# Causal attention and hard-swish MLP: the first loads in another order, and one small exponential at the start

## The chip, the cores and the metric

The kernel runs on one core of a Trainium2 chip. Its time is the device time of the whole program in microseconds (us). A core has TensorE (PE in the rows; PEld is its weight load), VectorE (DVE), ScalarE (ACT) and GpSimd (POOL), which compute, and SyncE (SP), which here issues every DMA. Each engine takes its instructions in the order in which the program lists them, and waits at the head of its list until the semaphores of that instruction are reached.

## The reference

```python
scores = q @ k^T / sqrt(64)                  # 4 batches, 12 heads, 448 x 64, causal mask
attn   = softmax(scores); x = attn @ v       # x laid out as 1792 tokens x 768
h      = x @ w_in                            # 768 -> 2048
out    = (h * clip(h + 3, 0, 6) / 6) @ w_out # 2048 -> 768
```

All is float32 at the border. The kernel keeps that accuracy by splitting x, the weights and the gated activations into a high and a low part and adding three matmuls (high by high, low by high, high by low).

## The kernel before

The 448 queries of a sequence are cut in four blocks of 112. **Group 0** is the first block of all four batches (448 tokens, made by `first_pair`, two heads at a time, six pairs p0 to p5); groups 1 to 4 are the other 336 queries of each batch (`pair`). Attention of a group must be done before its MLP (`group`). The MLP of a group is a long row of large matmuls on TensorE: 16 chunks of w_in (L598 to L600, 18 matmuls a chunk), then 24 of w_out.

A first pair goes through these steps: mask into two PSUM banks (L322), products of q and k (L329), on VectorE the row maximum of head 1 and of head 0 (L336, L342 between them) and the subtraction for head 0 (L356), on ScalarE the exponentials (L348 four times for head 1, L360 for head 0), on VectorE sum and inverse (L363, L369, L370), on GpSimd the scaling of both heads (L377), on TensorE the turn of both (L386), copies of the turned blocks (L238 on ScalarE or L241 on VectorE), the product with v (L399), and the split of x (L238 twice, then L250).

In group 0 the weights come as 64-bit words. VectorE turns every chunk of w_in (768 columns) into plain numbers in two halves of three instructions (L571, L573, L576) through a scratch PSUM bank; then ScalarE makes the high part (wh, L238), and GpSimd or VectorE the low part (wl, L250). The pairs of batch 0 in `pair` begin with their scores on TensorE (L453: two of 448 columns, two of 336, two of 224), each into a PSUM bank of its own, and then L476 on VectorE.

The order of all this is set by a planner in the kernel (`Flow.run`): each operation has a key (its due time, smaller first), estimated lengths and the buffers that it needs, and whenever an engine is free the planner gives it the ready operation with the smallest key. What comes out is one fixed list for each engine. PSUM has six banks tagged "s" (scores, attention, conversion scratch) and two tagged "mo" (turns, MLP sums). The DMAs of the first loads have keys from -900 on, so that they come first; equal keys go in the order in which they were written.

Of the kernel before, what the change touches and what calls it, by code (L numbers as in the profile page):

```python
# [32 lines left out]
F32 = mybir.dt.float32  # L33
F32R = mybir.dt.float32r
I32 = mybir.dt.int32
ACTF = mybir.ActivationFunctionType
# [154 lines left out]
def tile_causal_attention_hardswish_moe(ctx: ExitStack, tc: tile.TileContext, q, k, v, w_in, w_out, out):  # L191
    nc = tc.nc
# [12 lines left out]
    def buf(tag, shape, dt=F32):  # L205
        return Buf(tag, shape, dt)
# [4 lines left out]
    def ap(b):  # L211
        if b.tile is None:
            b.tile = pools[b.tag].tile(b.shape, b.dt, tag=b.tag, name=b.tag)
        return b.tile

    def f(x):
        return x.bitcast(F32)
# [35 lines left out]
    const = pools["const"]  # L253
# [2 lines left out]
    mask = const.tile([C, S], F32, tag="mask", name="mask")  # L256
    maskr = const.tile([C, B, C], F32R, tag="maskr", name="maskr")
    three = const.tile([128, 1], F32, tag="three", name="three")

    def setup():  # L260
        nc.vector.memset(ident, 1.0)
        nc.vector.memset(mask, 0.0)
        nc.vector.memset(three, 3.0)
        nc.gpsimd.affine_select(
            out=ident, in_=ident, pattern=[[-1, C]], base=0, channel_multiplier=1,
            compare_op=ALU.is_equal, fill=0.0,
        )
        nc.gpsimd.affine_select(
            out=mask[:, R:], in_=mask[:, R:], pattern=[[-1, C]], base=0, channel_multiplier=1,
            compare_op=ALU.is_ge, fill=-8.0e9,  # L270
        )
        nc.vector.tensor_copy(identr, ident)
        nc.vector.tensor_copy(maskr, mask[:, R:].unsqueeze(1).to_broadcast([C, B, C]))
# [17 lines left out]
    first_qk = buf("gh", [128, 2 * NPAIR, S])  # L291
    first_v = buf("gl", [128, NPAIR, S + 64])

    def by_batch(x):
        return x.rearrange("m (b s) -> m b s", b=B)

    def first_pair(p):
        t = T_FIRST + 8 * p
        for a, src in enumerate((q, k)):
            dma(  # L300
                -900 + 4 * p, 230e3, lambda a=a: by_batch(ap(first_qk)[:, 2 * p + a]),
                lambda src=src: src[:, p, :, :, :C].rearrange("b e d s -> (e d) b s"),
                w=[(first_qk, p, a)],
            )
# [239 lines left out]
    def cols(i):  # L544
        return 768 if i < NF else 512

    def weights(g, i, t, early):

        n = cols(i)
        wd, wh, wl = buf("wd", [128, 1536], I32), buf("wh", [128, 768], F32R), buf("wl", [128, 768], F32R)  # L550
        if g:
            dma(t - T_W - T_WLOAD, 512 * n, lambda: f(ap(wd))[:, :n], lambda: kept[i, :, :n], [("kept", i)], [(wd, 0)])
            w, wk = lambda: f(ap(wd))[:, :n], [(wd, 0)]
        else:
            m, r = divmod(i - NF, 4)
            src = w_in[i] if i < NF else w_out[m, :, 4 * r:4 * r + 4]
            dma(
                early if early else t - T_W - T_WLOAD, 1024 * n,
                lambda: ap(wd)[:, :2 * n].rearrange("p (n k) -> p n k", k=256), lambda: src, [], [(wd, 0)],
            )  # L560
            wf = buf("op", [128, 768])
            w = lambda: ap(wf)[:, :n]

            def bits(cv, o, m, step):
                ti = ap(cv)[:, :m].bitcast(I32)
                low, high = (ap(wd)[:, 2 * o + a:2 * o + 2 * m:2] for a in range(2))
                if step == 0:  # L570
                    nc.vector.tensor_scalar(ti, high, 3, 0x3FFFFFFF, ALU.logical_shift_left, ALU.bitwise_and)  # L571
                elif step == 1:
                    nc.vector.scalar_tensor_tensor(ti, high, -(1 << 30), ti, ALU.bitwise_and, ALU.bitwise_or)  # L573
                else:
                    o = ap(wf)[:, o:o + m].bitcast(I32)
                    nc.vector.scalar_tensor_tensor(o, low, 29, ti, ALU.logical_shift_right, ALU.bitwise_or)  # L576

            wk = []
            m = n if n <= 512 else n // 2
            for o in range(0, n, m):  # L580
                cv = bank("s")
                wk.append((wf, o))
                one_by_one = [
                    (elem(m), lambda _, cv=cv, o=o, a=a: bits(cv, o, m, a), [[(cv, 0)], [(cv, 0)], [(wf, o)]][a])
                    for a in range(3)
                ]
                flow.op(t - T_W + .01, {"D": (1, 0)}, one_by_one, [(wd, 0)] + ([("sums", NPAIR - 1)] if i else []))
            dma(t - T_W, 512 * n, lambda: kept[i, :, :n], w, wk, [("kept", i)])
        move(t - T_W + .1, n, lambda: ap(wh)[:, :n], w, wk, [(wh, 0)], {"A": 1})
        minus(  # L590
            t - T_W + .2, n, lambda: ap(wl)[:, :n], w, lambda: f(ap(wh))[:, :n], wk + [(wh, 0)], [(wl, 0)],
            {"D": 1.15, "P": (2, .5)} if g else {"P": 2, "D": (1.15, 2.0)},
        )
        return wh, wl
# [7 lines left out]
    def group(g):  # L602
        n, t0 = (R if g else S), 96 * g
        gh, gl = buf("gh", [128, NF, S], F32R), buf("gl", [128, NF, S], F32R)
        step = 6 * n * .4535e-3
        for i in range(NF):
            t = t0 + 3 * i
            wh, wl = weights(g, i, t, -900 + 4 * i + 11 if not g and i < 4 else None)
            acc, r = bank("mo"), buf("r", [128, S])
            for part in range(3):  # L610
                def products(part=part, wh=wh, wl=wl, acc=acc):
                    for c in (2 * part, 2 * part + 1):
                        xh, xl = (ap(x)[:, :n] for x in x_t[g, c])
                        triple(ap(acc)[:, :n], n, wh, wl, c, xh, xl, c == 0, c == NK - 1)
                cs = (2 * part, 2 * part + 1) if g else range(NK)
                xs = [(x, 0) for c in cs for x in x_t[g, c]]
                pe(t + part, [(step, products, [(acc, 0), ("step", t + part)])], [(wh, 0), (wl, 0)] + xs)
            t -= 4
            one(
                t, {"A": 1}, (n + 300) / 1200,  # L620
                lambda _, r=r, acc=acc: nc.scalar.activation(  # L621
                    ap(r)[:, :n], ap(acc)[:, :n], ACTF.Relu, bias=three, scale=1.0
                ),
                [(acc, 0)], [(r, 0)],
            )
            def gate(_, r=r, acc=acc):
                nc.vector.scalar_tensor_tensor(ap(r)[:, :n], ap(r)[:, :n], 6.0, ap(acc)[:, :n], ALU.min, ALU.mult)  # L627

            one(t, {"D": 1}, elem(n), gate, [(acc, 0)], [(r, 0)])
            move(  # L630
                t, n, lambda i=i: ap(gh)[:, i, :n], lambda r=r: ap(r)[:, :n], [(r, 0)], [(gh, i)],
                {"P": 1.05, "A": (1, .3)} if g else {"A": 1},
            )
            minus(
                t, n, lambda i=i: ap(gl)[:, i, :n], lambda r=r: ap(r)[:, :n], lambda i=i: f(ap(gh)[:, i, :n]),
                [(r, 0), (gh, i)], [(gl, i)], {"D": 1.4, "P": (2.6, 1.0)} if g else {"P": 2.3, "D": (1.4, 1.5)},
            )
        for m in range(NK):
            acc, ob = bank("mo"), buf("r", [128, S])
            for part in range(8):  # L640
                t = t0 + 48 + 8 * m + part
                if part % 2 == 0:
                    wh, wl = weights(g, NF + 4 * m + part // 2, t, None)

                def products(part=part, wh=wh, wl=wl, acc=acc):
                    for i in (2 * part, 2 * part + 1):
                        triple(
                            ap(acc)[:, :n], n, wh, wl, i % 4, ap(gh)[:, i, :n], ap(gl)[:, i, :n], i == 0, i == NF - 1
                        )
                gs = [(x, i) for i in (2 * part, 2 * part + 1) for x in (gh, gl)]  # L650
                pe(t, [(step, products, [(acc, 0), ("step", t)])], [(wh, 0), (wl, 0)] + gs)
            move(
                t + .5, n, lambda ob=ob: ap(ob)[:, :n], lambda acc=acc: ap(acc)[:, :n], [(acc, 0)], [(ob, 0)],
                {"A": 1, "D": (1.1, .5)}, 1.0 / 6.0,
            )
            rows = by_batch(out[128 * m:128 * m + 128])
            if g:
                dma(t + 1, 172e3, lambda rows=rows: rows[:, g - 1, C:], lambda ob=ob: ap(ob)[:, :n], [(ob, 0)])
            else:
                dma(t + 1, 230e3, lambda rows=rows: rows[:, :, :C], lambda ob=ob: by_batch(ap(ob)), [(ob, 0)])  # L660
# [49 lines left out]
```

## Time and profile before

| | us |
|---|---|
| median of 3 runs (lowest to highest) | 661.43 (659.28 to 661.99) |
| the profiled execution | 661.54 |
| its span | 659.8 |
| TensorE busy (share of the span) | 643.9 (98%) |
| VectorE, ScalarE, GpSimd busy | 465.8, 367.3, 301.2 |
| first matmul of group 0's MLP | 45.20 from the start of the span |

Busy times are sums over the span; TensorE has nearly all its idle time ahead of the first matmul of group 0's MLP. In the rows, a timeline line gives start and length, the engine, the line of the kernel, the operation and the tiles; the bracket says how long the engine stood idle before it and what ended the wait. Six q/k/v pair loads of 224 KB each (gh takes q and k, gl takes v) and four weight chunks of 768 KB (wd) are the first 22 transfers.

### The profile page before, as it was taken

To read this page: it belongs to the slowest core of one execution; us is meant where nothing else is said; L and a number is where in the kernel's file an instruction comes from. 1 tells how busy PE (TensorE), PEld (TensorE's weight loads), DVE (VectorE), ACT (ScalarE), POOL (GpSimd) and SP (SyncE) were. 2 spreads that over 40 slices of the span, in tenths; PEclk is the share of its full clock that TensorE was granted. 3 is DMA by queue.
4 is the path that set the end of the run, shared out by engine and by line. 5 is a ranking of instruction groups with operands and counts; after the bars stand their busy time and mean duration, and the time that the engine had idled before them with its cause. 6 is when DMAs were issued, how large, how long until landed. Compare 5 with 4: busy or idle time off the path is not lost.

```text
span 659.8 us, 12245 instructions
## 1 busy us (share of the span) xinstructions
PE 643.9 (98%) x4236; PEld 587.3 (89%) x4236; DVE 465.8 (71%) x939; ACT 367.3 (56%) x870; POOL 301.2 (46%) x333
## 2 busy tenths in 40 slices
PE   7689999999999999999999999999999999999998
PEld 5569887878889999999999999999999999999997
DVE  4889898977687798854588795567798743566432
ACT  3665656654546666555576664656666554444342
POOL 1667667546572686423375563433676410011100
PEclk9979999999999999999999999999999999999999
DMA  9989876888788543556744547555553334643452
GB/s 232 259 267 298 265 242 192 260 282 295 206 265 246 158 144 107 159 171 182 217 152 135 154 127 206 157 168 186 161 168 87 112 113 132 209 139 110 139 164 65
DMA packets 66878, 120.89 MB, mean 183 GB/s; under 512 B 16896, under 2 KB 33408, under 8 KB 66816
## 3 DMA queue, kind: packets, MB, share of 16 engines
q1 hardware_dynamic: 66816, 120.11, 60.7%
q8 instruction: 33, 0.54, 0.3%
q14 instruction: 29, 0.24, 0.1%
HBM read 101.99 MB, written 18.09 MB: 182 GB/s over the span
## 4 chain that ended last, share of the span: by engine, by line
PE 92%; DVE 3%; DMA 1%; SPq 1%; ACT 1%; POOL 1%; issue 1%; DVEq 0%; ACTq 0%; POOLq 0%
PE mo L598 24%; PE mo L600 23%; PE mo L599 23%; PE s L535 6%; PE s L516 6%; PE s L450 3%; PE s L451 2%; PE s L453 2%; DMA gh<-in_k_dram 1%; SPq L229 1%; PE s L399 1%; DVE s L571 1%; DVE s L573 1%; DVE op L576 0%; PE s L329 0%
## 5 line engine op out<-in xcount | busy, mean ns | idle before, releaser
L250 DVE TENSOR_TENSOR wl<-wd,wh 128x512 fp32r<-128x512 f32 (+1 forms) x159 | 142.8, 898 | 99.8 <-ACT wh L238 99.5
L238 ACT CAST wh<-wd 128x512 fp32r<-128x512 f32 (+1 forms) x160 | 112.9, 706 | 120.0 <-PE mo L599 85.9
L598 PE MATMUL mo<-xh,wh 128*128 128x336 f32 (+1 forms) x480 | 160.8, 335 | 0.1
L598 PE MATMUL mo<-gh,wh 128*128 128x336 f32 (+1 forms) x480 | 159.2, 332 | 0.0
L600 PE MATMUL mo<-xh,wl 128*128 128x336 f32 (+1 forms) x480 | 157.2, 327 | 0.0
L600 PE MATMUL mo<-gh,wl 128*128 128x336 f32 (+1 forms) x480 | 156.9, 327 | 0.3 <-POOL wl L250 0.3
L599 PE MATMUL mo<-gl,wh 128*128 128x336 f32 (+1 forms) x480 | 156.4, 326 | 0.0
L599 PE MATMUL mo<-xl,wh 128*128 128x336 f32 (+1 forms) x480 | 156.2, 325 | 0.0
L505 POOL TENSOR_SCALAR pr<-pr,prow 112x224 f32<-112x224 f32 x144 | 109.0, 773 | 39.5 <-DVE prow L493 39.3
L476 DVE CUSTOM_DVE_ANT_0 s<-s,mask 112x448 f32<-112x448 f32 (+1 forms) x144 | 70.6, 527 | 39.7 <-PE s L451 33.1
L245 POOL TENSOR_SCALAR gh<-r 128x336 fp32r<-128x336 f32 x51 | 33.3, 654 | 138.2 <-DVE r L627 128.6
L598 PEld LDWEIGHTS mo<-xh,wh 128*128 128x128 f32 x480 | 91.0, 190 | 5.8 <-issue 1.7
L598 PEld LDWEIGHTS mo<-gh,wh 128*128 128x128 f32 x480 | 90.3, 188 | 2.8 <-issue 0.8
L599 PEld LDWEIGHTS mo<-xl,wh 128*128 128x128 f32 x480 | 91.4, 190 | 1.1
L600 PEld LDWEIGHTS mo<-gh,wl 128*128 128x128 f32 x480 | 90.2, 188 | 2.2 <-POOL wl L250 0.6
L600 PEld LDWEIGHTS mo<-xh,wl 128*128 128x128 f32 x480 | 90.6, 189 | 1.3
L599 PEld LDWEIGHTS mo<-gl,wh 128*128 128x128 f32 x480 | 90.3, 188 | 1.3
L483 ACT ACTIVATE pr<-s,prow 112x448 f32<-112x448 f32 (+1 forms) x144 | 76.9, 542 | 25.7 <-DVE prow L476 25.7
L250 POOL TENSOR_TENSOR wl<-op,wh 128x512 fp32r<-128x512 f32 (+1 forms) x35 | 53.3, 1522 | 44.1 <-ACT wh L238 34.3
L238 ACT COPY pt<-s 112x336 f32<-112x336 f32 x139 | 53.3, 446 | 26.0 <-PE s L516 25.9
L621 ACT ACTIVATE r<-mo,three 128x336 f32<-128x336 f32 (+1 forms) x80 | 44.7, 558 | 26.4 <-PE mo L600 20.9
L245 POOL TENSOR_SCALAR op<-qk 128x784 fp32r<-128x784 f32 x31 | 30.4, 985 | 57.3 <-PE s L451 54.0
(70 smaller groups left out, 853.6 us busy)
## 6 DMA issues: line engine op xcount, KB each, us to landing
wd<-kept_w SPq DMA_DIRECT2D x64, 384.0 KB, 3.3
wd<-kept_w SPq DMA_DIRECT2D x96, 256.0 KB, 2.7
wd<-in_w_in_dram SPq DMA_DIRECT2D x16, 768.0 KB, 5.7
wd<-in_w_out_dram SPq DMA_DIRECT2D x24, 512.0 KB, 5.2
qk<-in_k_dram SPq DMA_DIRECT2D x84, 112.0 KB, 2.7
qk<-in_q_dram SPq DMA_DIRECT2D x84, 84.0 KB, 2.6
kept_w<-op SPq DMA_DIRECT2D x16, 384.0 KB, 5.7
kept_w<-op SPq DMA_DIRECT2D x24, 256.0 KB, 5.4
```

Of the source, the lines that this page charges most:

```text
L238: nc.scalar.copy(o(), i()) if scale is None else nc.scalar.mul(o(), i(), scale)
L245: nc.gpsimd.tensor_scalar(o(), i(), 1.0, 1.0, ALU.mult, ALU.mult)
L250: (nc.gpsimd if e == "P" else nc.vector).tensor_tensor(o(), a(), b(), ALU.subtract)
L476: lambda _, e=e, i=i, w=w, dst=dst: nc.vector.tensor_tensor_reduce(dst(), dst(), mask[:, S - w:], -0.125, 3.0e38, ALU.add, ALU.min, ap(st) ...
L483: lambda _, e=e, i=i, dst=dst: nc.scalar.activation(ap(pr[e, i]), dst(), ACTF.Exp, bias=ap(st)[:, e, i:i + 1], scale=-1.0, accum_out=ap(st ...
L505: nc.gpsimd.tensor_scalar(x, x, r, 1.0, ALU.mult, ALU.mult)
L516: nc.tensor.transpose(ap(tp)[:C, C * o:C * o + C], ap(pr[e, i])[:, C * j:C * j + C], ident)
L535: nc.tensor.matmul(ap(av)[64 * e:64 * e + 64, R - w:R], ap(vr)[:, j, e, :], ap(ph)[:, o:o + w], start=(j == 0), stop=(j == NC_ - 1),)
L598: nc.tensor.matmul(ps, ap(wh)[:, a], xh, start=start, stop=False)
L599: nc.tensor.matmul(ps, ap(wh)[:, a], xl, start=False, stop=False)
L600: nc.tensor.matmul(ps, ap(wl)[:, a], xh, start=False, stop=stop)
L621: lambda _, r=r, acc=acc: nc.scalar.activation(ap(r)[:, :n], ap(acc)[:, :n], ACTF.Relu, bias=three, scale=1.0),
```

## The change

The loads of q and k of pair p get the key -900 + 4p - 6, so that they stand 6 key units, a pair and a half, ahead of the load of v (-900 + 4p, as before). The four early weight chunks get the keys -883, -875, -871 and -867 in place of -889, -885, -881 and -877. And ScalarE computes one exponential of a 128 x 1 constant at the start, which pulls the load of its function table there.

```diff
+    warm = const.tile([128, 1], F32, tag="warm", name="warm")
 
     def setup():
         nc.vector.memset(three, 3.0)
+        nc.scalar.activation(warm, three, ACTF.Exp)
@@ first_pair: loads of q and k of pair p
-                -900 + 4 * p, 230e3, lambda a=a: by_batch(ap(first_qk)[:, 2 * p + a]),
+                -900 + 4 * p - 6, 230e3, lambda a=a: by_batch(ap(first_qk)[:, 2 * p + a]),
@@ group: key of the load of weight chunk i
-            wh, wl = weights(g, i, t, -900 + 4 * i + 11 if not g and i < 4 else None)
+            wh, wl = weights(g, i, t, -900 + (17 if not i else 21 + 4 * i) if not g and i < 4 else None)
```

The lines of the new file stand two further down than those of the old one (L329 is L331 there, L598 is L600).

Since the planner reads the landing of a load as the time from which work is ready, the lists of all engines change. The first places, on SyncE, are the loads themselves; before:

```order
L229 DMA gh<-in_q_dram 128x4x112
L229 DMA gh<-in_k_dram 128x4x112
L229 DMA gl<-in_v_dram 112x4x128
L229 DMA gh<-in_q_dram 128x4x112
L229 DMA gh<-in_k_dram 128x4x112
L229 DMA gl<-in_v_dram 112x4x128
L229 DMA gh<-in_q_dram 128x4x112
L229 DMA gh<-in_k_dram 128x4x112
L229 DMA gl<-in_v_dram 112x4x128
L229 DMA wd<-in_w_in_dram 128x1536
L229 DMA gh<-in_q_dram 128x4x112
L229 DMA gh<-in_k_dram 128x4x112
```

And now:

```order
L229 DMA gh<-in_q_dram 128x4x112
L229 DMA gh<-in_k_dram 128x4x112
L229 DMA gh<-in_q_dram 128x4x112
L229 DMA gh<-in_k_dram 128x4x112
L229 DMA gl<-in_v_dram 112x4x128
L229 DMA gh<-in_q_dram 128x4x112
L229 DMA gh<-in_k_dram 128x4x112
L229 DMA gl<-in_v_dram 112x4x128
L229 DMA gh<-in_q_dram 128x4x112
L229 DMA gh<-in_k_dram 128x4x112
L229 DMA gl<-in_v_dram 112x4x128
L229 DMA gh<-in_q_dram 128x4x112
```

The k of pairs p1, p2, p3 and p5 was transfer 5, 8, 12 and 20, and is now 4, 7, 10 and 16; weight chunk 0 was transfer 10 and is now 18.

On TensorE the list begins, before, with masks (L322), products (L329) and the turn of pair p0 (L386, its two heads pr_215 and pr_225):

```order
L322 MATMUL s<-maskr,identr 112x448 x6
L329 MATMUL s<-gh 112x112 x16
L322 MATMUL s<-maskr,identr 112x448 x2
L329 MATMUL s<-gh 112x112 x8
L322 MATMUL s<-maskr,identr 112x448 x2
L386 MATMUL mo<-ident,pr_215 112x112 x4
L386 MATMUL mo<-ident,pr_225 112x112 x4
```

Eight products are one pair, so x16 is p0 and p1, and the next eight p2. Now (the same operations at L324, L331 and L388):

```order
L324 MATMUL s<-maskr,identr 112x448 x6
L331 MATMUL s<-gh 112x112 x24
L324 MATMUL s<-maskr,identr 112x448 x2
L331 MATMUL s<-gh 112x112 x8
L324 MATMUL s<-maskr,identr 112x448 x2
L388 MATMUL mo<-ident,pr_225 112x112 x4
L388 MATMUL mo<-ident,pr_227 112x112 x4
```

The products of p3 and the masks of p4 now stand between the products of p2 and the turn of p0. (One set of masks moved from ahead of p2's products to behind them.)

The third place is on TensorE where group 0's MLP begins. Before, its first matmul stands right behind the product with v of the last pair, p5 (s_590):

```order
L399 MATMUL s_590<-pt0_577,gl_144 64x112
L399 MATMUL s_590<-pt0_544,gl_144 64x112
L598 MATMUL mo_624<-xh_323,wh_399 128x448
L599 MATMUL mo_624<-xl_346,wh_399 128x448
L600 MATMUL mo_624<-xh_323,wl_413 128x448
```

Now, with the semaphores that each row waits for (s_584 is the product with v of p5):

```order
L401 MATMUL s_584<-pt0_578,gl_148 64x112
L401 MATMUL s_584<-pt0_553,gl_148 64x112
L455 MATMUL s_609<-qk_186 112x448 [waits DMAHW5_49,DMAHW3_49]
L455 MATMUL s_611<-qk_186 112x448 [waits DMAHW6_49,DMAHW4_49,Activation_49]
L455 MATMUL s_618<-qk_186 112x336 [waits DVE_49,PE_49]
L455 MATMUL s_620<-qk_186 112x336 [waits PE_49,Activation_49]
L455 MATMUL s_626<-qk_186 112x224 [waits Activation_49]
L455 MATMUL s_628<-qk_186 112x224 [waits DVE_49]
L600 MATMUL mo_645<-xh_329,wh_448 128x448
L601 MATMUL mo_645<-xl_344,wh_448 128x448
L602 MATMUL mo_645<-xh_329,wl_473 128x448
```

The six scores of the second pair of batch 0 (L455), which before stood among the matmuls of group 0, have moved ahead of its first one. By the values of the semaphores in the two programs, s_618 waits for the first half, and s_628 for the second half, of the conversion of weight chunk 2 on VectorE, since they take over its PSUM scratch banks (s_593 and s_614). That stands on VectorE, behind the copy of p5's turned block (pt0_553) and chunk 1, as

```order
L241 COPY pt0_553<-mo_536 112x448
L573 TENSOR_SCALAR s_558<-wd_173 128x384
...
L578 SCALAR_TENSOR_TENSOR op_570<-wd_173,s_576 128x384
L573 TENSOR_SCALAR s_593<-wd_175 128x384
L575 SCALAR_TENSOR_TENSOR s_593<-wd_175,s_593 128x384
L578 SCALAR_TENSOR_TENSOR op_603<-wd_175,s_593 128x384
L478 ISA s_523,prow_495<-s_523,mask_123 112x224
L478 ISA prow_495 112x1
L573 TENSOR_SCALAR s_614<-wd_175 128x384
L575 SCALAR_TENSOR_TENSOR s_614<-wd_175,s_614 128x384
L578 SCALAR_TENSOR_TENSOR op_603<-wd_175,s_614 128x384
```

(wd_173 is chunk 1, wd_175 chunk 2; six rows of conversion are one chunk.)

On VectorE, too, the subtraction for p2 (L356, now L358) waits for the turn of p0, in both programs, because its result takes p0's buffer, of which there are four.

## Rows read from the trace of the kernel before

**Rows 1.** Waits of TensorE in the whole execution: waiter, releaser, us, times, longest.

```profile
PE s L516 <- ACT pt L238: 0.4, 1, 0.4
PE mo L600 <- POOL wl L250: 0.3, 1, 0.3
```

**Rows 2.** Timeline, first us: start, length, engine, line, operation, tiles, count [idle before].

```profile
7.69 1.28 ACT L348 ACT_TABLE_LOAD   x1 [7.69 <-DVE prow L342]
13.87 1.82 POOL L377 TENSOR_TENSOR pr<-pr,prow 112x448 f32<-112x448 f32 x2 [12.00 <-DVE prow L370]
```

**Rows 3.** Timeline of the DMA issues: the seventh and the ninth transfer.

```profile
4.16 0.49 SPq L229 DMA_DIRECT2D gh<-in_q_dram  x1
5.61 1.58 SPq L229 DMA_DIRECT2D gl<-in_v_dram  x1
```

**Rows 4.** DMA issues with us to landing, at 4.16 (q) and at 5.61 (v).

```profile
gh<-in_q_dram SPq DMA_DIRECT2D x1, 224.0 KB, 6.8
gl<-in_v_dram SPq DMA_DIRECT2D x1, 224.0 KB, 7.5
```

**Rows 5.** Timeline of TensorE before group 0; x8 or x16 is one merged set.

```profile
13.78 1.09 PE L322 MATMUL s<-maskr,identr 112*112 112x448 f32 x2
14.85 1.89 PE L386 MATMUL mo<-ident,pr 112*112 112x112 f32 x8
17.23 1.84 PE L329 MATMUL s<-gh 64*112 64x112 f32 x16 [0.49 <-DMA gh<-in_k_dram]
33.62 2.96 PE L453 MATMUL s<-qk 64*112 64x448 f32 x8
44.28 0.99 PE L399 MATMUL s<-pt,gl 112*64 112x112 f32 x16 [1.80 <-ACT pr L483]
```

**Rows 6.** Timeline of TensorE from the first matmul of group 0.

```profile
45.20 0.48 PE L598 MATMUL mo<-xh,wh 128*128 128x448 f32 x1
45.91 0.56 PE L598 MATMUL mo<-xh,wh 128*128 128x448 f32 x1
49.25 0.41 PE L598 MATMUL mo<-xh,wh 128*128 128x448 f32 x1
72.01 1.57 PE L453 MATMUL s<-qk 64*112 64x448 f32 x8
74.92 0.64 PE L453 MATMUL s<-qk 64*112 64x224 f32 x4
```

**Rows 7.** Timeline of VectorE: parts of a first pair, scores, two halves of a conversion.

```profile
6.78 0.62 DVE L336 TENSOR_REDUCE prow<-s 112x4 f32<-112x448 f32 x1 [4.49 <-PE s L329]
8.16 0.62 DVE L356 TENSOR_TENSOR pr<-s,prow 112x448 f32<-112x448 f32 x1
12.66 0.61 DVE L363 TENSOR_REDUCE prow<-pr 112x4 f32<-112x448 f32 x1
16.85 0.62 DVE L356 TENSOR_TENSOR pr<-s,prow 112x448 f32<-112x448 f32 x1 [0.53 <-PE mo L386]
40.98 0.62 DVE L476 CUSTOM_DVE_ANT_0 s<-s,mask 112x448 f32<-112x448 f32 x1
46.32 0.60 DVE L571 TENSOR_SCALAR s<-wd 128x384 int32<-128x384 int32 x1
48.02 0.55 DVE L571 TENSOR_SCALAR s<-wd 128x384 int32<-128x384 int32 x1
```

**Rows 8.** Timeline of GpSimd: the low half of weight chunk 0.

```profile
27.09 1.85 POOL L250 TENSOR_TENSOR wl<-op,wh 128x768 fp32r<-128x768 f32 x1 [3.21 <-ACT wh L238]
```

**Rows 9.** Groups of VectorE instructions by line and shape, 60 to 200 us.

```profile
L250 DVE TENSOR_TENSOR wl<-op,wh 128x768 fp32r<-128x768 f32 x3 | 3.1, 1028 | 0.0
```

**Rows 10.** Stretches: length, busy us of VectorE (instructions), granted clock, DMA share, GB/s.

```profile
6.70:49.70 43.00, 35.13 (x79) 0.88 0.98 265
34.00:38.00 4.00, 2.83 (x8) 0.50 0.69 199
46.00:49.00 3.00, 2.90 (x7) 0.50 1.05 382
```

## The prediction

> **What bounds the kernel now.** I read the list of TensorE's waits first. From the middle of group 0 on there are two, of 0.4 and 0.3 us, in some 600 us [rows 1]: once group 0's MLP runs, the program lasts as long as TensorE's list. So the time is the moment of that MLP's first matmul, 45.20 us [rows 6], plus a remainder that the change can hardly touch. What it can touch lies before 45.20, and I read that stretch as a timeline, TensorE first, then VectorE. The reader is to see that VectorE is the fullest engine there (35.1 of 43.0 us [rows 10]) and TensorE the one that makes it wait: TensorE works much of this stretch at the lower of its levels (1.2 and 2.4 GHz). The granted clock is 0.50 in 34 to 38 us [rows 10], and the first four of a pair's six scores, 2.96 us there [rows 5], take 1.57 later [rows 6].
>
> **Loads.** Transfers land almost in the order of issue. The seventh was issued at 4.16 and took 6.8 us, the ninth at 5.61 and took 7.5 [rows 3, 4]: 11.0 and 13.1, so 1.07 us for each load of 224 KB. The k of p2 is now the seventh (11.0) and that of p3 the tenth (14.2), where the wait for p3's k ended only at 17.23 before [rows 5]. The k of p5 (sixteenth) comes at about 20.6. This is a gain only where somebody waits for it.
>
> **Table load.** 1.28 us at 7.69, at the head of ScalarE's first exponentials [rows 2], now at the start, beside SyncE's first issues and VectorE's memsets. p0's exponentials come that much earlier. But VectorE now does p1's maxima and subtraction (2.0 us, from 6.78 to the end of the row at 8.16 [rows 7]) before p0's sums and inverse (1.2 us, from 12.66 to GpSimd's start at 13.87 [rows 7, 2]). With p1's products at 9.5, GpSimd scales p0 from 12.8 instead of 13.87: 1.1 us gained. The Trainium skill, "ScalarE: Activation LUTs", section "What ACT_TABLE_LOAD costs", adds a drain of about 1.38 us to the 1.28 us load, 2.66 together. By that the scaling could be 1.4 us earlier still. The sum below is the same by both, because of the next step.
>
> **The first turn.** p0's turn used to start at 14.85 and take 1.89 [rows 5]; VectorE's subtraction for p2, which needs p0's buffer, followed at 16.85 [rows 7]. Now p3's products and p4's masks stand ahead of the turn. TensorE: p2's products from 11.0, 1.84; masks 1.09, to 14.0; p3's k at 14.2, products 1.84, to 16.0; masks 1.09, to 17.1; turn 1.89, to 19.0 (all at the lengths of [rows 5]). The subtraction comes 2.1 us later than before, although its data are ready at 15.5. So the gain of the loads and of the table is not only hidden, it is turned round here.
>
> **VectorE from 19.0.** Its list goes on without a long wait, since the products of p3 and p4 are there: subtraction of p2 0.62; p3 and p4 2.0 each; two copies, the size of a subtraction, 1.24; sums and inverse of p2 to p4, 1.15 each, 3.45; maxima of p5 1.4; the two halves of weight chunk 0, 1.70 each (46.32 to 48.02 [rows 7]), 3.4. That is 14.1, and with some 0.4 of short waits it ends at 33.5. The inverse of p3, 0.5 before that, starts GpSimd's scaling (half of 1.82) and TensorE's turn of p3 (half of 1.89 at the lower clock), for whose buffer the subtraction of p5 waits: 35.1. Behind it: 0.62, the low part of chunk 0 1.03 [rows 9], a sum 0.61, two L476 at 0.6 [rows 7], an inverse 0.5, together 4.0, to 39.1. TensorE meanwhile: second turn of p3 0.95, four scores 2.96, product with v 0.99 [rows 5] at the high level or twice that, taken as 1.4, first turn of p4 0.7 between both levels: 41.1. That is what VectorE's next copy waits for. Then copy 0.62, three smaller L476 (estimate 1.4, from 0.62 for the large one), p5's copy 0.62, to 43.7; chunks 1 and 2, four halves, 6.8, with one L476 of 0.4 between: 50.9.
>
> **The new wait.** The second pair's last score needs the scratch bank of chunk 2's second half, so it starts at 50.9, and group 0's matmuls stand behind it on TensorE: first matmul at 51.2 against 45.20. Queued with it are all 18 matmuls of chunk 0, whose own operands are there long before (in the old trace the low part of chunk 0 is done at 28.9 [rows 8]). Would they not pass it? The row at 44.28 says no: TensorE stood 1.80 us idle before a product with v [rows 5], with the operands of group 0's first matmuls present. The Trainium skill, "PSUM — Partial Sum Buffer", section "Engine vs sequencer instructions", says that matmuls start and complete in program order; the trace agrees with it here. Were it not so, the first matmul would come at about 47.
>
> **Sum.** First matmul 6.0 later. The six scores brought forward no longer stand inside the MLP, where they took 1.57 and 0.64 [rows 6]: -2.2. Clock: in the old trace the nine matmuls from 45.91 to 49.25 took 0.37 each at a granted 0.50 [rows 6, 10], which cost half of 3.3, 1.7 us, after the idle of 1.80. In the new one TensorE does little between 44 and 51, so I expect the same loss again; bounds are none (-1.7) and twice it (+1.7), and I take +0.5, nearer to the old row. VectorE enters the MLP with chunks 0 to 2 and two pairs' scores nearly done, so the old 0.7 of waits [rows 1] may shrink: -0.4. Together +3.9 on the profiled execution's 661.54 (span 659.8 and 1.7 around it): 665.4. The median of the runs, 661.43, differs by 0.1.
>
> Ends of the unknown: if VectorE never waits after 19.0, its 14.1 + 4.0 + 2.6 + 7.2 end at 46.9, and the first matmul is at 47.2; with the clock loss and all waits gone, 661.54 - 0.2 - 1.7 - 0.7 = 658.9. If TensorE stays at the low level (first matmul 52.0), the loads come 1 us later and the clock loss doubles: 661.54 + 53.0 - 45.2 - 2.2 + 1.7 = 668.8.
>
> **Rivals.**
> *No change.* TensorE works almost without a gap from 11.0 on, and might reach its high level by about 17 and keep it. Then mask and turn save 1.4 of the way to 19.0, the scores 1.4, and TensorE is ready before VectorE everywhere behind: 17.6 + 14.1 + 0.4, p3's scaling and turn 1.2, 4.0, 2.6, 7.2, first matmul 47.4. That is 2.2 later than before, the very 2.2 of the scores: 661.5. For it: the old list had TensorE waiting for loads just there. Against it: VectorE's short waits would have to vanish.
> *Faster.* The high level already for p3's products. Then p0's turn is bound by p3's k alone: 14.2 + 1.0 + 0.6 + 0.9 = 16.7, VectorE runs on without waits (2.3 before 46.9), first matmul at 44.9, and the clock is up when it starts: -0.3 - 2.2 - 1.7 = -4.2, 657.3. It decides from a first matmul before 47.4. Against it: the set at 17.23 still took 1.84 after three earlier sets had run [rows 5].
> *The load that was put back.* Weight chunk 0 is now transfer 18. The seventeenth lands at 21.7, and 768 KB at the rate of the small loads add 3.7: 25.4. VectorE gets there at about 26.6. If the transfers lose 3 us, VectorE waits 2 more: 667.4.
>
> **How the numbers follow.** Forecast 0.55, no change 0.30, faster 0.08, late chunk 0.07. About 0.5% (3.3 us) is what a measurement can tell from no change: slower begins at 664.8. Four fifths of the forecast's share and the late chunk lie beyond it: 0.52. Within: the no-change case and the forecast's lower fifth, 0.40. Faster: 0.08. The range, 660.0 to 668.6, holds the forecast with its upper bound and the no-change case; outside stay the faster rival and the extremes.
>
> **What would show it.** Right: an ACT_TABLE_LOAD in the first 2 us; p3's products ahead of p0's turn and the subtraction of p2 near 19; TensorE idle before the last score of 224 columns, released by VectorE's L578; the first group-0 matmul near 51, and then no waits. Wrong: that first matmul before 48, or the conversion of chunk 2 done before p5's product with v, which would mean that I have VectorE's waits too long; or a wait of the conversion on the load of chunk 0.

## The result and the profile after

| | before | after |
|---|---|---|
| median of six runs each, us | 660.94 (659.28 to 661.99) | 669.99 (666.09 to 672.2) |
| ratio, 95% interval | 1 | 1.0138 (1.0102 to 1.0173) |
| profiled execution, its span, us | 661.54, 659.8 | 672.2, 670.2 |
| first matmul of group 0's MLP, us | 45.20 | 49.01 |

The change costs 9 us; 3.9 us were forecast. (The times here and below are of executions at the usual speed; one of the seven of e5 took 1600.83 us and is left out.) To see where the time goes I numbered the 2880 MLP matmuls of each trace in their order of start (they are the same in every kernel here) and subtracted the start in the trace before. The first is 3.81 us late, the 127th (at about 80 us) 2.30, and it stays at that to 130 us. The last is 10.45 late. So 2.3 us of this execution stand in the front (the program up to the first stretch of group 0's MLP), on which nearly the whole prediction was spent, and 8.2 us in the late part behind it, where the prediction saw nothing that the change could reach.

**The front.** The table load now stands at the start of ScalarE, as forecast. ScalarE's first rows (start, length, engine, line, operation, tiles, idle before):

```profile
0.79 1.28 ACT L265 ACT_TABLE_LOAD   x1 [0.79 <-PEq L701]
2.08 0.20 ACT L265 ACTIVATE warm<-three 128x1 f32<-128x1 f32 x1
7.70 0.35 ACT L350 ACTIVATE pr<-s,prow 112x112 f32<-112x112 f32 x1 [5.41 <-DVE prow L344]
```

The exponential behind it starts 0.01 us after the end of the load. The Trainium skill, "ScalarE: Activation LUTs", section "What ACT_TABLE_LOAD costs", adds a drain of some 1.38 us to the load; this row shows none. TensorE's rows from p2's products to p0's turn, and from p5's product with v to the first group-0 matmuls:

```profile
9.82 1.34 PE L331 MATMUL s<-gh 64*112 64x112 f32 x16 [1.56 <-DMA gh<-in_k_dram]
12.42 1.84 PE L331 MATMUL s<-gh 64*112 64x112 f32 x16 [0.24 <-DMA gh<-in_k_dram]
15.07 1.70 PE L388 MATMUL mo<-ident,pr 112*112 112x112 f32 x8
...
43.18 0.99 PE L401 MATMUL s<-pt,gl 112*64 112x112 f32 x16 [1.40 <-ACT pt L238]
44.10 1.01 PE L455 MATMUL s<-qk 64*112 64x448 f32 x4
46.08 1.48 PE L455 MATMUL s<-qk 64*112 64x336 f32 x6 [0.98 <-DVE op L578]
48.00 1.08 PE L455 MATMUL s<-qk 64*112 64x224 f32 x2 [0.44 <-DVE op L578]
49.01 0.74 PE L600 MATMUL mo<-xh,wh 128*128 128x448 f32 x1
```

The new wait is there: the six scores of the second pair stand ahead of group 0's first matmul, and the last ones wait for VectorE's conversion (L578). But the product with v is at 43.18, 1.1 us earlier than in [rows 5], and p0's turn is at 15.07, not 17.1: the products of p2 and p3, which waited for their loads, started 1.2 and 1.8 us before the forecast's 11.0 and 14.2. VectorE's subtraction for p2 is at 16.88, as in [rows 7]. The clock, by the windows (length, busy time and count of each engine, granted clock, DMA share, GB/s):

```profile
6.70:49.70 43.00, 31.13 (x256) 21.84 (x257) 34.18 (x84) 26.93 (x91) 21.40 (x21) 0.78 0.94 262
46.00:49.70 3.70, 3.18 (x10) 1.76 (x11) 3.60 (x12) 1.99 (x6) 3.35 (x4) 0.76 1.05 310
49.70:55.00 5.30, 5.30 (x17) 4.66 (x16) 3.50 (x8) 1.26 (x6) 3.76 (x6) 0.52 0.87 295
```

At 0.52 the group's first matmuls take 0.37 us each to 54.8; before, that stretch ended at 49.3 [rows 6].

**The late part.** TensorE's waits from 55 us on (in total, times, longest), which before were 0.7 us [rows 1], and VectorE's longest waits in 160 to 215 us:

```profile
PE mo L600 <- DVE r L629: 2.5, 3, 1.6
PE s L452 <- DVE op L250: 2.3, 1, 2.3
PE mo L602 <- POOL wl L250: 0.7, 1, 0.7
PE mo L600 <- ACT wh L238: 0.6, 1, 0.6
PE s L518 <- ACT pt L238: 0.3, 1, 0.3
PE s L518 <- POOL pr L507: 0.3, 1, 0.3
```

```profile
DVE op L578 <- DMA kept_w<-op: 10.6, 5, 4.3
DVE kl L250 <- ACT op L238: 3.7, 1, 3.7
```

TensorE's waits are 6.7 us, 6.0 more than before, and that is all of its idle time behind the 127th matmul. The other 2 us or so are matmuls that follow each other more slowly without a wait in the list: over the 480 from the 481st on (179 to 297 us) it is 2.4 us, those waits left out, and little elsewhere. Why, I did not find out. VectorE's wait, 10.6 us for landed stores, is 2.4 in the same stretch before:

```profile
DVE op L576 <- DMA kept_w<-op: 2.4, 2, 1.8
```

It is for one kind of buffer:

```python
BUFS = dict(... op=3, ...)
wf = buf("op", [128, 768])          # a converted weight chunk of group 0, until it is stored (kept_w) and split
op, kl = [[buf(a, [128, w], F32R) for _ in qk] for a, w in (("op", R + S), ("kl", S))]   # a pair of groups 1 to 4
```

The three "op" buffers hold converted chunks, and for each head of a pair of groups 1 to 4 the high part of q and k, until its scores are done. The two copies of the first group-1 pair (op<-qk, 128x784), GpSimd's and ScalarE's rows after, then GpSimd's before:

```profile
163.32 0.85 POOL L245 TENSOR_SCALAR op<-qk 128x784 fp32r<-128x784 f32 x1
...
203.17 0.85 ACT L238 CAST op<-qk 128x784 fp32r<-128x784 f32 x1 [3.39 <-DMA kept_w<-op]
```

```profile
160.97 0.85 POOL L245 TENSOR_SCALAR op<-qk 128x784 fp32r<-128x784 f32 x1
...
167.44 0.85 POOL L245 TENSOR_SCALAR op<-qk 128x784 fp32r<-128x784 f32 x1
```

Before, the second head follows 6.5 us behind the first, the scores are done, both buffers come free. After, it comes 39.9 us later: in the new list the chunks took the other two buffers each time, so the first head's half keeps one for 40 us, and the conversions go round on two, each waiting for the landing of a store. VectorE's rows:

```profile
178.88 0.69 DVE L578 SCALAR_TENSOR_TENSOR op<-wd,s 128x512 int32<-128x512 int32 x1 [3.92 <-DMA kept_w<-op]
...
191.23 0.69 DVE L578 SCALAR_TENSOR_TENSOR op<-wd,s 128x512 int32<-128x512 int32 x1 [4.34 <-DMA kept_w<-op]
...
204.05 0.62 DVE L250 TENSOR_TENSOR kl<-qk,op 128x448 fp32r<-128x448 f32 x1 [3.74 <-ACT op L238]
```

Theory A: the planner laid the list anew from the first loads to the end, and its late part fell badly; neither the loads nor the front cost these 8 us. A2, in the expectations, is its closer form: the heads of one pair are split far apart, and the first of them keeps a buffer from the conversions. Rivals: the transfers themselves (L), or a late loss that follows from the late front (F).

### The profile page after: what moved, and what is told of

Read it like the earlier page. It is cut to its first block, busy times and chain, and to the rows that moved or that the text cites. A ratio compares the mean times of both kernels' runs of the same rounds, so it can differ in the third digit from the quotient of the medians.

```text
span 670.2 us, 12240 instructions
## 1 busy us (share of the span) xinstructions
PE 646.1 (96%) x4236; PEld 587.1 (88%) x4236; DVE 462.8 (69%) x935; ACT 368.4 (55%) x873; POOL 304.2 (45%) x335
## 4 chain that ended last, share of the span: by engine, by line
PE 87%; DVE 4%; POOL 4%; issue 2%; DMA 1%; SPq 1%; ACT 1%; POOLq 0%; DVEq 0%; ACTq 0%
PE mo L600 23%; PE mo L602 22%; PE mo L601 22%; PE s L537 6%; PE s L518 6%; PE s L452 3%; PE s L453 2%; POOL pr L507 2%; PE s L455 2%; DMA gh<-in_k_dram 1%; SPq L229 1%; PE s L401 1%; PE mo L388 1%; DVE s L478 1%; POOL gh L245 1%
## 5 line engine op out<-in xcount | busy, mean ns | idle before, releaser
L250 DVE TENSOR_TENSOR wl<-wd,wh 128x512 fp32r<-128x512 f32 (+1 forms) x155 | 137.3, 886 | 101.9 <-ACT wh L238 99.2
L600 PE MATMUL mo<-xh,wh 128*128 128x336 f32 (+1 forms) x480 | 162.1, 338 | 1.9 <-DVE r L629 1.9
L600 PE MATMUL mo<-gh,wh 128*128 128x336 f32 (+1 forms) x480 | 159.8, 333 | 1.2 <-DVE r L629 0.7
L600 PEld LDWEIGHTS mo<-xh,wh 128*128 128x128 f32 x480 | 91.4, 190 | 8.0 <-DVE r L629 3.2
L600 PEld LDWEIGHTS mo<-gh,wh 128*128 128x128 f32 x480 | 90.3, 188 | 4.7 <-ACT wh L238 2.0
L245 POOL TENSOR_SCALAR gh<-r 128x336 fp32r<-128x336 f32 x49 | 29.3, 598 | 141.5 <-DVE r L629 140.1
```

Of the source, the lines that this page charges most:

```text
L245: nc.gpsimd.tensor_scalar(o(), i(), 1.0, 1.0, ALU.mult, ALU.mult)
L250: (nc.gpsimd if e == "P" else nc.vector).tensor_tensor(o(), a(), b(), ALU.subtract)
L600: nc.tensor.matmul(ps, ap(wh)[:, a], xh, start=start, stop=False)
```

## The experiments

All ratios are against the kernel before on the same chip in the same session (medians 660.08 to 661.14). The offsets are those of the numbered matmuls, from one profiled execution each; the late part is the last offset less the 127th; the last column is the time between the two copies op<-qk of the first group-1 pair.

| kernel | median us | ratio (95%) | first group-0 matmul | 127th matmul | last | late part | two heads apart |
|---|---|---|---|---|---|---|---|
| after | 669.99 | 1.0138 (1.0102-1.0173) | 49.01 | +2.30 | +10.45 | 8.2 | 39.9 |
| e1 old list, new loads | 664.42 | 1.0064 (1.0049-1.0080) | 49.04 | +3.09 | +2.87 | -0.2 | 6.4 |
| e2 new list, old loads | 673.25 | 1.0202 (1.0187-1.0217) | 54.26 | +4.87 | +11.61 | 6.7 | 37.6 |
| e3 before, plan nudged | 666.34 | 1.0095 (1.0079-1.0111) | 44.19 | -1.29 | +4.67 | 6.0 | 37.9 |
| e5 after, 4 op buffers | 664.53 | 1.0084 (1.0045-1.0123) | 48.16 | -1.21 | +3.74 | 5.0 | 34.4 |
| e6 old list, q and k ahead | 660.25 | 0.9990 (0.9978-1.0002) | 44.79 | -0.93 | -1.07 | -0.1 | 6.5 |
| e7 scores behind | 666.48 | 1.0080 (1.0056-1.0104) | 46.24 | +4.44 | +6.05 | 1.9* | 7.3 |
| e8 early exponential alone | 659.66 | 0.9979 (0.9969-0.9989) | 44.58 | -1.40 | -1.62 | -0.2 | 6.4 |
| e9 replanned, 4 buffers | 665.74 | 1.0077 (1.0055-1.0099) | 44.57 | -3.08 | +2.66 | -0.5* | 24.1 |
| e10 weights at old places | 668.42 | 1.0126 (1.0108-1.0143) | 45.84 | +0.80 | +8.91 | 4.9* | 2.5 |
| e11 after, nudged back | 660.38 | 1.0010 (0.9988-1.0031) | 47.02 | -2.37 | -1.83 | 0.5 | 4.2 |
| e12 e8, nudged | 659.63 | 0.9985 (0.9973-0.9997) | 43.45 | -2.28 | -2.69 | -0.4 | 6.4 |
| e13 after, pairs later | 659.71 | 0.9993 (0.9973-1.0013) | 46.73 | -4.70 | -4.06 | -0.9* | 0.8 |

(*) In the lists of e7, e9, e10 and e13 other attention matmuls stand ahead of the 127th than before, so its offset is not time won or lost. For these four I counted the work of all kinds of matmul done by 100 us, each at its mean length behind 80 us; by that they stand 4.2, 3.1 and 4.0 us behind the kernel before at 100 us, and e13 3.2 ahead, good to some 0.5 us, and the late part is what comes behind.

**e1 and e2: list and loads exchanged.** The loads are emitted ahead of the list, in an order of their own (in short):

```diff
-        for _, _, e, emit in order: emit(e)
+        for _, _, emit in sorted(loads, key=lambda x: x[:2]): emit("SP")   # first 22, by the other kernel's keys
+        for _, _, e, emit in order:                                        # list of the one kernel
+            if emit not in ahead: emit(e)
```

> The list of the kernel before on every engine, with only the first 22 loads in the changed order and the one early exponential. Theory A (the new list, and not the transfers, costs the time): the first group-0 matmul stays at 44 to 45.5 us, the stretch from 150 to 300 us looks as before, and the time is 659.5 to 661.9 us. Rival L (the changed order of the transfers itself costs it, by late v blocks or weight chunks): 665 to 670 us.

> The list of the changed kernel on every engine, with the first loads in the old order and without the early exponential. Theory A: as slow as the changed kernel or 1 to 2 us slower, since products of p2 and p3 now wait for their loads: 669 to 673 us, with VectorE's waits for the stores of converted chunks at 178 to 200 us still there. Rival L: 660 to 663 us.

The late loss goes with the list: none in e1, 6.7 us in e2, whose loads are the old ones. So do VectorE's waits for stores in 160 to 215 us, in e1 and then in e2 (whose lines stand about ten and eight further down than before):

```profile
DVE op L586 <- DMA kept_w<-op: 2.0, 2, 1.1
```

```profile
DVE op L584 <- DMA kept_w<-op: 9.4, 5, 3.8
```

But e1 is not at 659.5 to 661.9, and rival L is right on the front. The old list has VectorE convert chunk 0 at 17.93; now its load lands 18th. VectorE's longest wait from 10 to 30 us (L581 is the first step of the conversion), and TensorE's masks for p4 that wait behind it:

```profile
DVE s L581 <- DMA wd<-in_w_in_dram: 6.1, 1, 6.1
```

```profile
24.04 1.09 PE L331 MATMUL s<-maskr,identr 112*112 112x448 f32 x2 [5.67 <-DVE op L586]
```

**e3: nothing but the plan.** A number of the kernel before that only the planner uses:

```diff
-    DMA_RATE, DMA_LATENCY = 260e3, 2.5
+    DMA_RATE, DMA_LATENCY = 260e3, 2.6
```

> The kernel before, in which only the planner's assumed latency of a load is 2.6 instead of 2.5; no load, buffer or instruction is changed, and the list is the same up to about 150 us. Theory A2 (late in group 0 the list hangs on chance: a small shift of the plan lets the operand split of a group-1 pair hold one of the three op buffers for 40 us, and VectorE waits for stores): front as before (first group-0 matmul 45.2), TensorE loses 5 to 7 us between 180 and 260 us, time 666 to 668.5 us. Rival F (what is lost late is a consequence of the later front): 661 to 662 us.

Met in the time and the late loss; the first matmul came 1.0 us earlier than expected. The list is the one before to about 150 us, yet the late part loses 6.0 us. TensorE's listed waits there are 4.7 us, 4.0 more than before, and VectorE waits for the same buffer:

```profile
DVE op L576 <- DMA kept_w<-op: 9.5, 4, 3.9
```

```profile
PE mo L598 <- DVE r L627: 2.5, 3, 1.6
PE s L450 <- DVE op L250: 1.6, 1, 1.6
```

This rules out F: here the front is even 1.3 us early, and in e1, where it is 3.1 late, nothing is lost behind it.

**e5: four op buffers.** The planner still counts three, so the list is that of after:

```diff
-    for tag, bufs in dict(const=1, **BUFS).items():
+    for tag, bufs in {"const": 1, **BUFS, "op": 4}.items():
```

> The changed kernel's list, instruction for instruction, with four op buffers on the chip instead of three. Theory A2: VectorE's 10.6 us of waits for landed stores (178 to 200 us) fall below 3 us, TensorE's 7 us of waits in 190 to 270 us fall below 2, time 663.5 to 665.5 us, which leaves the 2.3 us of the front. Rival S (the stores stand late in SyncE's queue, behind a load of v that waits for TensorE): the waits stay, 669 to 670 us.

The time is met, but by luck. VectorE's wait for stores falls from 10.6 to 1.7 us, yet the late part only from 8.2 to 5.0; the rest comes from the front, which in this execution of the same list stood at -1.2 us instead of +2.3. The second head's copy still has the copies of nine chunks ahead of it in ScalarE's list, and TensorE waits for a gate (L629, the product of h with its clipped part):

```profile
DVE op L578 <- DMA kept_w<-op: 1.7, 1, 1.7
```

```profile
PE mo L600 <- DVE r L629: 3.8, 4, 2.3
```

So the buffer is some 3 of the 8 us directly. The other 5 stay with this order of the list: 4.2 us of waits, 3.5 more than before, and behind the longest of them, from 203.8 us, 3.5 us at a granted clock of 0.51, worth some 1.7. Which place in the list makes them was not tried by itself.

**e6 and e8: the parts without a new plan.** e6 is e1 with chunk 0 as the 12th load and the others between the blocks; e8 is before with the exponential alone, the lines `warm` of the change's diff.

```diff
-                             -900 + (17 if not i else 21 + 4 * i) if not g and i < 4 else None)   # place in e1
+                             -900 + (9 if not i else 11 + 4 * i) if not g and i < 4 else None)    # place in e6
```

> The list of the kernel before, q and k of each block one turn ahead of v, and the early exponential, as in the run of the old list with all new loads; but weight chunk 0 is the 12th load instead of the 18th and the other chunks stand between the blocks. Theory B (that run lost its time only where VectorE stood 6.1 us at the late weight chunk): that wait falls below 1 us, the first group-0 matmul comes at 42.5 to 45.0, time 657 to 660 us. Rival V (VectorE's own work sets the front, so that earlier q and k give nothing): first group-0 matmul 45 to 45.5, 660 to 661.5 us. Rival L (transfers in this order cost time in themselves): 663 us or more.

> The kernel before with the early exponential alone; list and loads are its own. Theory H (the table load is hidden): within 0.7 us of the kernel before. Rival T (p0's scaling 1.1 us earlier goes through to the MLP): 1.0 to 1.4 us faster.

e6: the wait for chunk 0 is down to 0.7 us, as theory B had it, but q and k ahead of v give nothing beyond e8. The time is rival V's, the first matmul, 44.79, still in theory B's range; that VectorE sets the front, as V says, is not shown by it. e8: rival T's size, faster by 1.4 us (0.7 to 2.0). It is not p0's scaling, which starts at 13.71 instead of 13.87; the gain comes later, where TensorE's product with v and the turns behind it run shorter. Before, then in e8:

```profile
19.00 1.76 PE L399 MATMUL s<-pt,gl 112*64 112x112 f32 x16
20.69 1.60 PE L386 MATMUL mo<-ident,pr 112*112 112x112 f32 x8
```

```profile
18.34 1.31 PE L401 MATMUL s<-pt,gl 112*64 112x112 f32 x16
19.58 0.98 PE L388 MATMUL mo<-ident,pr 112*112 112x112 f32 x8
```

The granted clock reads 1.00 from 16 to 22 us in both, so it doesn't tell why. What the table load has to do with that I cannot show, and one profile of each doesn't tell it from chance; the 1.4 us rest on 12 and 23 executions.

**e7 and e9: the new wait.** e7 makes the second pair's scores wait for group 0's first 18 matmuls:

```diff
-                    raw, True,
+                    raw + ([("step", 0)] if p == 1 else []), True,
```

e9 adds four op buffers known to the planner, the weight chunks' old places, other due times (T_EARLY 8, T_REST -12, T_W 11, T_WLOAD 8) and a latency of 1.5.

> The changed kernel, with the six scores of the second batch-0 pair held behind group 0's first 18 matmuls; the list is laid anew from there, and in it both heads of the first group-1 pair are split close together. Theory W (the wait for the conversion of chunk 2 delays the MLP's start): first group-0 matmul 44 to 45 instead of 49.0, around 100 us the matmuls stand 0 to 1 us behind the kernel before instead of 2.3; and with three op buffers free late in group 0 TensorE loses under 3 us there: 660 to 663 us. Rival N (VectorE would be late anyway, TensorE waits a few us later instead): still 2 to 3 us behind at 100 us, 663 to 666 us.

> A combination: q and k one turn ahead, the early exponential, weight chunks at their old places, the six scores held behind group 0's first 18 matmuls, four op buffers that the planner knows of, and other times for the pairs and weight chunks, so that no operand split waits for a buffer late in group 0. Theory A2 and W together: first group-0 matmul 43.5 to 45, no TensorE wait over 1 us behind it, 655 to 658.5 us. Rival (something that the plan doesn't see takes it back, as SyncE's queue): 660 us or more.

Both missed; e7 lies beyond rival N, and e9 came to its rival's time. The first matmul comes 2.8 and 4.4 us earlier than in after, and TensorE then waits for VectorE's gate of the first chunks, longest at 57.36 in e7 and at 55.96 in e9 (e7's waits from 45 us on, then e9's):

```profile
PE mo L600 <- DVE r L629: 3.3, 2, 2.7
```

```profile
PE mo L600 <- DVE r L629: 3.9, 1, 3.9
```

The scores ahead of the MLP were no loss by themselves: TensorE waits for VectorE there in one place or in the other. In e7 the two heads are split 7.3 us apart, and the late part costs 1.9 us, as theory A had it. In e9 they are 24.1 us apart and the late part costs nothing: with a fourth buffer that the plan knows of, the distance does no harm.

**e10 and e11: the changed kernel nudged.** e11 is after with another planner's latency; e10 the same with the weight chunks at their old places among the loads.

```diff
-    DMA_RATE, DMA_LATENCY = 260e3, 2.5
+    DMA_RATE, DMA_LATENCY = 260e3, 2.0
```

> The changed kernel, in which only the planner's assumed latency of a load is 2.0 instead of 2.5: loads, buffers and early exponential are the changed kernel's, and TensorE's list is the same over its first 500 rows and differs late in group 0. Theory A2 (of the 10.5 us, 8 come from how the list happens to fall late in group 0): front as in the changed kernel (first group-0 matmul 49, 2.3 us behind the kernel before at 100 us), VectorE's waits for landed stores in 160 to 215 us below 6 us instead of 10.6, time 664 to 667 us. Rival F (the late loss follows from the late front): 669 to 671 us.

> The same with the weight chunks at their places of before among the loads (so only q and k ahead and the early exponential remain of the change). Theory C (the front's 2.3 us come from weight chunk 0 landing as the 18th load, round which the planner moves the conversions to a later place in VectorE's list): first group-0 matmul 44 to 46, 1 us ahead to 0.5 us behind the kernel before at 100 us. Rival Q (q and k ahead of v are what reorders VectorE's list and costs the front): 2 us or more behind at 100 us. The end depends on how the list falls late in group 0: 662 to 667 us.

e11 is the sharpest run: same loads, same exponential, the same order of instructions on all five engines to about 130 us, and 660.38 us. The late part costs 0.5 us, with VectorE waiting 1.4 us for stores:

```profile
DVE op L578 <- DMA kept_w<-op: 1.4, 1, 1.4
```

The time is below the expected 664 to 667, since the front too came out otherwise: the 127th matmul is 2.37 us early instead of 2.30 late. The instructions are the same; the clock is not. The window of e11 that answers to that of after:

```profile
46.00:49.70 3.70, 3.26 (x16) 2.79 (x16) 3.60 (x12) 2.70 (x7) 3.35 (x4) 1.00 1.05 362
```

1.00 here, 0.76 there and 0.52 in the 5 us behind. Together with e5 these are three executions of one front, at +2.30, -1.21 and -2.37. So +2.3 is one draw of the front, not its price.

e10 doesn't decide between C and Q (first matmul at 45.84 as C said, some 4 us behind at 100 us as Q said) and missed its time. It also limits the buffer theory: its heads are 2.5 us apart, and the late part still costs some 4.9 us. That stands in 176 to 190 us, where the turns of a pair follow each other in TensorE's list and wait for copies, 2.2 us in all, and a granted clock of 0.76 means 6.7 of the 14 us at the lower level, worth at most 3.4:

```profile
PE s L518 <- ACT pt L238: 1.2, 2, 0.7
PE s L452 <- ACT pt L238: 0.5, 1, 0.5
PE s L518 <- ACT pr L485: 0.5, 1, 0.5
```

```profile
176.00:190.00 14.00, 11.73 (x59) 8.37 (x58) 10.92 (x22) 7.30 (x19) 4.20 (x5) 0.76 0.73 216
```

**e12 and e13: good draws on purpose.** e12 is e8 with a planner's latency of 2.2, e13 is after with `T_EARLY` (the due time of batch 0's pairs) 8 instead of 4.

> The kernel before with the early exponential, and a planner's latency of 2.2 instead of 2.5, which changes the list a little late in group 0 and nowhere before. Theory A2 (late in group 0 the list is a draw, and the draw of the kernel before is already a good one, with 0.7 us of TensorE's waits in all): as the early exponential alone, 0.7 to 2 us below the kernel before, no operand split that holds its buffer over 20 us. Rival (any new draw there costs some us): 662 us or more.

> The changed kernel with batch-0 pairs keyed 4 later (8 instead of 4), which lays the list anew from about 60 us on; its front is the changed kernel's to the first group-0 matmul. In this list the two heads of the first group-1 pair are split 2.5 us apart, not 40. Theory A2: late loss 0 to 2 us, time 659.5 to 663. Rival F (the changed front costs 2 us or more, and the late loss follows from it): 667 us or more.

Both as theory A said. From 55 us on TensorE waits once in e12 and once in e13:

```profile
PE s L518 <- ACT pt L238: 0.4, 1, 0.4
```

```profile
PE s L537 <- ACT pt L238: 0.2, 1, 0.2
```

e13 carries the whole change and is some 10 us faster than it, by a list that falls otherwise from 60 us on, and with its front in a better draw (first matmul at 46.73). The fastest in ratio are e8 and e12, both below the kernel before and the changed one.

Taken together: that the list, and not the loads or the front, makes the late loss is shown by e1, e2, e3 and e11. How it makes it is shown in part: the held buffer is worth some 3 us by e5, and e10 loses late without it.

## Why the prediction was wrong

The direction was right, and more by luck than by its steps; the size was wrong, 665.4 against 669.99.

- **What bounds the kernel: this step failed.** "The time is the moment of that MLP's first matmul, 45.20 us, plus a remainder that the change can hardly touch." The remainder took 8.2 of the 10.45 us between the two profiled executions. That TensorE waits 0.7 us in 600 is a property of one list, not of the kernel: late in group 0 conversions, stores, operand copies and turns are tight, and e3 shows that the same front with another plan loses 6.0 us there. The change of keys had the planner lay the whole list anew, and the argument treated only its front.
- **Loads.** Order as forecast, moments 1.2 to 1.8 us too late.
- **Table load.** Place and length as forecast. p0's scaling, forecast for 12.8, came at 11.83, since p1's products ended at 8.26, not 9.5. The gain was called lost in the first turn; alone, by e8, the exponential is worth 1.4 us, but not by the earlier scaling that was reckoned with.
- **First turn.** Forecast to push p2's subtraction to 19.0; it came at 16.88, since p3's products started at 12.42, not 14.2. Nothing was turned round there.
- **VectorE from 19.0, and the new wait.** The wait exists, at the place named, with VectorE's L578 as its end; the first matmul came at 49.01, not 51.2. But in e7, without it, TensorE waits 2.7 us a little later, so it is no loss of its own.
- **Sum.** +6.0 for the first matmul was +3.8; -2.2 for the scores moved was -2.75 (offset 5.05 at the 91st matmul, 2.30 at the 127th); +0.5 for the clock was +1.2 (from 3.81 at the first matmul to 5.05 at the 91st, the first short stalls included). So the front's three terms, +4.3, were +2.3 in this execution, and e11 with the same list had -2.4: the sum was smaller than what moves between two executions of the same instructions. The -0.4 for fewer stalls was +8.2, of which 6.0 are waits.
- **Rivals.** Late chunk 0 was priced at 2 us and given 0.07. With the old list it costs 4 to 5 us (e1 against e6); the new plan converts it from 24.24 on, and VectorE has no wait for a load there. The rival that was not there is that a new list loses elsewhere. (In the working, the 35.1 is 0.2 above its terms, and 0.52 and 0.40 are 0.01 off; neither matters.)

## What to carry to other kernels

Where a planner lays out a whole program, a change of a few keys is a new draw of everything behind it: compare the list to its end, and above all who holds each small pool, before saying that a far stretch is untouched. Change the loads with the list held fixed (as e1 and e6 do) to learn what the loads are worth, and nudge a number of the planner that means nothing (e3, e11) to learn how much a draw is worth: here 6 and 10 us, more than any part of the change. And it may pay not to let two operands that are needed together take buffers one by one from a pool that a stream of other work also uses; no run here tried that alone.

## What was not expected of the hardware

The same instructions ran at other granted clocks in the first 55 us: between after and e11, with the same list there, the 127th MLP matmul differs by 4.7 us, of which 2.0 are there at the first one (49.01 and 47.02) and the rest falls while matmuls take 0.37 us in the one and 0.20 in the other. e11's row behind the one above:

```profile
49.70:55.00 5.30, 5.30 (x28) 4.96 (x28) 5.07 (x10) 2.34 (x4) 4.48 (x7) 1.00 1.04 388
```

The Trainium skill, "TensorE: Matmul & The Clock Gate", section "Part 1: The HAM clock gate", says that the low level is the default and activity releases it. The trace agrees in that the low of after at 0.52 follows the waits at 43 to 48 us; why e11, with the same two waits for VectorE (1.4 us), has 1.00 there no row shows. The clock of whole executions tells the same of one program: e5's six took 661.9 to 663.8 us at a mean granted clock of 0.990 or more, 665.3 at 0.985, and 670.0 and 670.9 at 0.982 and 0.980. The kernel before shows no such thing: its 23 executions beside e8 lie between 658.6 and 662.6 us, at 0.981 as at 0.997. So a difference of some 5 us between two profiles of the new front says nothing about the change.

SyncE held a store back: the issue at 185.47 was ready when its conversion ended at 183.45, but the load of v ahead of it at 184.61 waited for TensorE.

```profile
180.02 0.44 SPq L229 DMA_DIRECT2D kept_w<-op  x1
184.61 0.33 SPq L229 DMA_DIRECT2D vr<-in_v_dram  x1
185.03 0.38 SPq L229 DMA_DIRECT2D wd<-in_w_out_dram  x1
185.47 0.43 SPq L229 DMA_DIRECT2D kept_w<-op  x1
```

Of the 4.34 us that VectorE stood before 191.23, when this store had landed, some 2.0 are this, if an earlier issue had landed as much earlier.
